# Row statistics by two ScalarE passes, turns from 128 rows, and a new order of instructions, in a gated linear attention with an MLP

## The chip, the cores and the metric

The kernel runs on one core of one Trainium2 chip. The time is that of the device, in microseconds, and the median of 3 runs of the kernel before is 220.5 us (219.09 to 223.66). Engines are named as in the profile: PE is TensorE, DVE VectorE, ACT ScalarE, POOL GpSimd, SP SyncE. A profile comes from one further execution, whose own time is given with it.

## The reference

Batch 4, 8 heads, 768 steps, 48 columns a head; x has 4 x 768 rows of 384 columns.

```python
def _attn_ref(q, k, v, a_re, a_im):
    mag = np.sqrt(a_re * a_re + a_im * a_im)
    scale = np.minimum(mag, 0.999) / (mag + 1e-06)
    a_re_n, a_im_n = (a_re * scale, a_im * scale)
    for t in range(S):
        new_re = ar * S_re - ai * S_im
        new_im = ar * S_im + ai * S_re
        S_re, S_im = (new_re + outer(k[t], v[t]), new_im)
        y[:, :, t] = np.einsum('bhd,bhde->bhe', q[:, :, t], S_re)

def _moe_ref(x, g_ln, w_ch1, w_ch2):
    mu = np.mean(x, axis=-1, keepdims=True)
    var = np.mean((x - mu) ** 2, axis=-1, keepdims=True)
    xn = (x - mu) / np.sqrt(var + 1e-06) * g_ln
    return x + np.maximum(xn @ w_ch1, 0.0) @ w_ch2
```

## The kernel before

The 4 x 768 rows are cut into 24 chunks of 128 rows (six a batch). Chunks are worked in 9 groups: chunk 0, chunks 1 and 2, and then seven groups of three. Per group, the gates come first. Under one ACT table (natural log and exp), `gate_exp` takes the log of a_re, the ratio r = a_im / a_re, and from both the log of the magnitude (lm), which is capped; a matmul with a triangular matrix sums it down the rows (`l_ps`), and two exp passes give the factors `epn`. Under the other table (trig), `gate_trig` takes the arctangent of r; matmuls sum the angles in turns (`th_ps`), and ACT takes sine and cosine. The whole group's q and k are multiplied by the factors (`qke`, L581) and by sine and cosine (`stk`, L587). The two tables alternate, 12 loads of them in all (L369). The first phase (a pair of loads) holds the first two groups, the second to fourth one group each, and the last two two groups each.

Per chunk, `attention` turns q and k (on PE for chunks 0 to 11, by DMA from SP for 12 to 23), takes the scores (`a_ps`), masks them (`at`), gets `y_ps` from them, v and the carried state s, and copies it to `x` in bf16 (L669). `feed` takes mean and variance of each row of x (L723, L724), turns x (`x_ps`, `xt`), multiplies by the first weights (`h_ps`), applies relu (`ht`, L767 on ACT and L769 on DVE), multiplies by the second weights (`o_ps`), scales by the reciprocal root of the variance (`rs`, three chunks at once, on POOL, L728 and L729), adds x (L786) and stores. The mean is taken out in the weights themselves: at the start `centre` is built from g_ln, and `fold` multiplies it into the first weights.

Nothing is scheduled by the program at run time: every operation is an entry of a plan, and two tables fix what happens. `HOW` names the engine of each of the operations that have a choice (V is DVE, A is ACT, P is POOL; a string has one letter for each group, chunk, or half of a chunk), and its `'order'` (L51) lists the numbers of all 806 operations in the order in which they are emitted. Each engine, and each queue of DMAs on SP and POOL, works off its own part of that list strictly in order. `'fill'` (L89) says before which results PE runs idle matmuls with the identity (`filled`, L173). The microseconds in `op`, `opt` and `act` are the planner's costs; they do nothing when `'order'` is given.

The lines that the change touches:

- L723 and L724: `bn_stats` and `bn_aggr` on DVE, whose second column of `mv` is the variance; L728 adds 1e-6 to it, L729 raises it to -0.5.
- L669: the copy of `y_ps` to `x`, on ACT for 10 chunks and on DVE for 14.
- L529: the whole turns. A matmul of a one-row tile `ones` with a one-row tile `rows` (192 turns, or 768 for chunks 3 to 5 of the first batch) starts each sum of angles, and L531 and L533 add to it with 128-row matrices. L262 and L263 fill `rows`.
- L738: the copy of `x_ps` to `xt`, on DVE.

Of the kernel before, what the change touches and what calls it, by code (L numbers as in the profile page):

```python
# [10 lines left out]
FP32 = mybir.dt.float32  # L11
# [37 lines left out]
 'xt': 'PPPPPPPPPPPPDDDDDDDDDDDD',  # L49
 'qkt': 'PPPPPPPPPPPPDDDDDDDDDDDD',  # L50
 'order': [12, 27, 41, 221, 13, 10, 23, 11, 25, 4, 1, 7, 35, 15, 5, 37, 59, 57, 53, 202, 222, 223, 51, 234, 209, 235,  # L51
# [37 lines left out]
 'fill': {209: 6.42, 229: 1.25, 242: 0.23, 249: 2.72, 494: 0.37, 496: 1.33, 779: 0.34}}  # L89
# [35 lines left out]
def kernel(  # L125
# [38 lines left out]
    def filled(ps):  # L164
# [5 lines left out]
        else:  # L170
            n = min(ps.shape[1], 512) // C
            for _ in range(int(us / (0.003 + n * 0.0534))):
# [13 lines left out]
             (2, ("dec",)), (4, ("edge",)), (6, ("carry",))] + [(2, ("in_" + n,)) for n in ("ar", "ai", "q", "k", "v")]  # L186
# [38 lines left out]
    def load(eng, g0, g1, names, after=()):  # L225
        b, c0, c1 = g0 // NCH, g0 % NCH, g0 % NCH + g1 - g0
        us = 0.6 if eng is Y else 0.66 + 0.26 * (c1 - c0)
# [50 lines left out]
    def constants():  # L278
# [5 lines left out]
        for name, us, fn, a in (("ones", 0.17, plain, (1.0,)),  # L284
                                ("all_turn", 0.17, plain, (INV2PI,)), ("all_back", 0.17, plain, (-INV2PI,)),
                                ("near", 0.86, shifts, (0, 192.0)), ("far", 0.86, shifts, (32, 768.0))):
            op(V, us, [], [("c_" + name,)], fn, name, *a)
        op(V, 0.23, [("c_u_turn",), ("c_all_turn",)], [("c_back",)], back)
        op(V, 0.3, [], [("c_small",)], small)
# [93 lines left out]
    def gate_exp(G):  # L383
# [67 lines left out]
        fp = lambda p: dict(V=0.48, A=0.52, P=p)  # L451
# [6 lines left out]
        if ratio:  # L458
# [3 lines left out]
            each("r", dict(V=0.48, P=0.95), ["ai"], [("rec", g)], "r", e_r, [in_("ai")])  # L462
            opt("r2", g, dict(V=0.06 + 0.215 * n, A=sb, P=0.06 + 0.69 * n), [("r", g)], [("r2", g)], e_r2, port=True)
            act(sb, [("r2", g), ("c_small",)], [("m2", g)], e_l1p, uses=[("rec", g)])
            op(V, 0.06 + 0.42 * n, [("ln", g), ("m2", g)], [("lm", g)], e_both, uses=[rw], port=True)
        else:
            each("ar2", fp(0.82), ["ar"], [], "ar2", e_ar2, [in_("ar")])
            each("ai2", fp(0.82), ["ai"], [], "m2", e_ai2, [in_("ai")])
            each("m2", dict(V=0.48, P=0.95), [], [("ar2", g), ("m2", g)], "sum", e_m2, [in_("ar")])
            act(sb, [("ar2", g)], [("ln", g), rw], e_ln, uses=[in_("ar")])  # L470
            act(sb, [("ln", g)], [("rw", rw[1], "rec")], e_rec, uses=[rw])
            each("r", dict(V=0.48, P=0.95), ["ai"], [("rw", rw[1], "rec")], "r", e_r, [in_("ai"), rw])
# [13 lines left out]
    def gate_trig(G):  # L486
# [20 lines left out]
        for j in (js[::-1] if G["back"] else js):  # L507
# [4 lines left out]
            elif (j != js[0] if G["back"] else j != js[-1]) or (G["b"] == 0 and G["c0"] + j < NCH - 1):  # L512
                key = ("carry", next(sums))
                opt("carry", c, dict(V=0.36, P=0.36), [last[1], ("th", g)], [key], e_add, last[0], j, key, port=True, **kw)
                last = ((lambda key=key: cell[key]), key)
# [340 lines left out]
```

## Time and profile before

| what | us |
|---|---|
| median of 3 runs | 220.5 |
| time of the profiled execution | 218.88 |
| its span | 217.1 |
| POOL busy (93 instructions) | 100.9 |
| 12 ACT table loads, each | 1.283 |
| granted PE clock, mean | 0.976 |
| masking of scores, L641, 24 of DVE | 29.1 |

The span runs from the first to the last instruction. Busy time of an engine is the time in which one of its instructions was running. A row of a group gives the count, the busy time, the mean duration of one in ns, and the idle time of the engine just before them with what ended it. The chain is found by going back from the last instruction, at each step to whatever released it, so that its pieces add up to the span.

### The profile page before, as it was taken

What the parts mean: (1) busy time and instruction counts of PE and PEld (TensorE: products, weight loads), DVE (VectorE), ACT (ScalarE), POOL (GpSimd) and SP (SyncE); (2) the same over time, 40 slices, a digit from 0 to 9 for tenths busy, and PEclk for the clock granted to TensorE, in tenths of its full rate; (3) what the DMA queues carried; (4) which work ended last, traced back from release to release, by engine and by line L of the source; (5) the groups of instructions that cost most, each with busy time, mean ns of one, the idle gap of its engine ahead of it and who ended that gap; (6) DMA issues with size and microseconds to landing.
All of it is one profiled execution on the core that took longest, in us unless ns stands there. A gap on an engine that the chain in (4) does not pass through costs nothing.

```text
span 217.1 us, 5425 instructions
## 1 busy us (share of the span) xinstructions
PE 187.7 (86%) x2292; PEld 134.6 (62%) x2295; DVE 177.9 (82%) x297; ACT 128.9 (59%) x161; POOL 100.9 (46%) x93
## 2 busy tenths in 40 slices
PE   3997695879789989997988889787999999899992
PEld 1333342658666976757866646567876677787871
DVE  4372779799999898999999967997968998888671
ACT  2259674929778797939988867528698511110100
POOL 4089997494966976346992800760060100020200
PEclk9999979999999999999999957999999999999999
DMA  6999999999799999999999929798349499792202
GB/s 109 180 165 109 189 150 157 145 198 156 65 143 139 215 180 202 189 143 248 162 78 201 198 27 211 135 146 136 92 101 138 92 219 177 182 156 57 92 3 109
DMA packets 136885, 31.45 MB, mean 145 GB/s; under 512 B 129948, under 2 KB 135772, under 8 KB 136860
## 3 DMA queue, kind: packets, MB, share of 16 engines
q0 software_dynamic: 78192, 14.16, 84.8%
q1 hardware_dynamic: 58668, 16.93, 39.2%
q8 instruction: 18, 0.29, 0.6%
q14 instruction: 7, 0.06, 0.1%
HBM read 28.31 MB, written 4.72 MB: 152 GB/s over the span
## 4 chain that ended last, share of the span: by engine, by line
PE 34%; DVE 27%; ACT 12%; DMA 11%; POOL 5%; issue 5%; SPq 3%; DVEq 0%; ACTq 0%; POOLq 0%
PE o_ps L782 13%; PE h_ps L761 11%; DMA qkt<-stk 5%; DVE at L641 5%; DVE lm L424 3%; SPq L214 3%; DVE w L546 3%; DMA ai<-in_a_im_dram 2%; DVE stk L587 2%; ACT epn L442 2%; ACT r L492 2%; DMA out_dram<-o 2%; DVE ht L769 2%; DMA xt<-x 2%; DVE r L390 2%
## 5 line engine op out<-in xcount | busy, mean ns | idle before, releaser
L761 PE MATMUL h_ps<-xt,w1c 128*128 128x128 bf16 x864 | 55.4, 220 | 2.8 <-DMA xt<-x 1.3
L761 PEld LDWEIGHTS <-w1c 128*128 128x128 bf16 x864 | 50.6, 98 | 4.6 <-issue 2.4
L782 PE MATMUL o_ps<-w2b,ht 128*128 128x384 bf16 x288 | 51.5, 331 | 0.0
L782 PEld LDWEIGHTS <-ht 128*128 128x128 bf16 x288 | 27.6, 99 | 17.3 <-issue 1.2
L767 ACT ACTIVATE ht<-h_ps 128x1024 bf16<-128x1024 f32 (+1 forms) x30 | 24.1, 820 | 23.4 <-PE h_ps L761 14.4
L641 DVE TENSOR_TENSOR at<-a_ps,mask 128x1024 bf16<-128x1024 f32 x24 | 29.1, 1216 | 2.8 <-PE a_ps L637 2.6
L728 POOL TENSOR_SCALAR rs<-mv 128x3 f32<-128x3 f32 x8 | 3.7, 464 | 56.0 <-DVE mv L724 37.2
L390 POOL TENSOR_TENSOR r<-ai,m 128x384 bf16<-128x384 f32 x13 | 13.5, 1058 | 21.8 <-ACT m L411 12.7
L442 ACT ACTIVATE epn<-l_ps 128x384 bf16<-128x384 f32 (+1 forms) x32 | 18.6, 658 | 6.2 <-PE l_ps L437 6.2
L786 DVE SCALAR_TENSOR_TENSOR o<-o_ps,rs,x 128x384 f32<-128x384 f32 x24 | 14.6, 613 | 8.9 <-PE o_ps L782 4.8
L769 DVE TENSOR_SCALAR ht<-h_ps 128x512 bf16<-128x512 f32 (+1 forms) x18 | 16.5, 921 | 1.8 <-PE h_ps L761 1.7
L581 POOL TENSOR_TENSOR epn<-qk,epn 128x1152 bf16<-128x1152 bf16 (+2 forms) x7 | 14.4, 2064 | 7.5 <-ACT epn L442 7.0
L637 PE MATMUL a_ps<-qkt 128*128 128x128 bf16 x192 | 14.8, 220 | 3.4 <-DMA qkt<-stk 2.0
L612 PE MATMUL qk_ps<-ident,stk 128*128 128x128 bf16 x192 | 13.4, 219 | 4.8 <-DVE stk L587 4.5
L369 ACT ACT_TABLE_LOAD x12 | 15.4, 1283 | 0.9 <-PEq L840 0.7
L612 PEld LDWEIGHTS <-stk 128*128 128x128 bf16 x192 | 11.4, 98 | 6.7 <-DVE stk L587 5.4
L546 DVE TENSOR_SCALAR w<-th_ps 128x384 f32<-128x384 f32 (+1 forms) x16 | 11.7, 749 | 4.2 <-ACT sin L543 4.1
L637 PEld LDWEIGHTS <-qkt 128*128 128x128 bf16 x192 | 11.6, 98 | 5.6 <-DMA qkt<-stk 2.2
L663 PE MATMUL y_ps<-v,at 128*128 128x48 bf16 x192 | 12.4, 183 | 1.8 <-DVE at L641 1.8
L173 PEld LDWEIGHTS <-ident 128*128 128x128 bf16 x55 | 6.2, 117 | 12.4 <-issue 5.3
L408 ACT ACTIVATE rec<-ar 128x1152 f32<-128x1152 f32 (+2 forms) x9 | 9.4, 1054 | 7.4 <-DMA ar<-in_a_re_dram 7.4
L543 ACT ACTIVATE sin<-th_ps 128x384 bf16<-128x384 int16 (+1 forms) x14 | 8.8, 645 | 8.0 <-PE th_ps L533 6.2
(102 smaller groups left out, 374.2 us busy)
## 6 DMA issues: line engine op xcount, KB each, us to landing
out_dram<-o SPq DMA_DIRECT2D x24, 192.0 KB, 7.0
ai<-in_a_im_dram SPq DMA_DIRECT2D x12, 192.0 KB, 5.0
ar<-in_a_re_dram SPq DMA_DIRECT2D x12, 192.0 KB, 7.0
ar<-in_a_re_dram POOLq DMA_DIRECT2D x2, 1152.0 KB, 13.4
ai<-in_a_im_dram POOLq DMA_DIRECT2D x2, 1152.0 KB, 12.1
qk<-in_k_dram POOLq DMA_DIRECT2D x3, 576.0 KB, 10.6
qk<-in_q_dram POOLq DMA_DIRECT2D x3, 576.0 KB, 10.8
v<-in_v_dram POOLq DMA_DIRECT2D x3, 576.0 KB, 8.6
```

The costliest lines, as they stand in the source:

```text
L369: op(A, 1.28, old, [key], lambda: A.preload_act_table_set(TABLES[which]))
L390: times = lambda eng, out, x, y: eng.tensor_tensor(out=out, in0=x, in1=y, op=ALU.mult)
L442: A.activation(out=o, in_=banks(G["l_ps", j], m), func=AF.Exp, scale=(1.0, -1.0)[s])
L546: V.tensor_scalar(out=cols(f32(G, "w"), j, m), in0=banks(G["th_ps", j], m), scalar1=0.25, scalar2=None, op0=ALU.add)
L612: T.transpose(ps[:, h], G["stk"][:, int(which == "ks"), j, ts(h, C)], K["ident"])
L637: T.matmul(ch["a"][:, h], lhsT=ch["kt"][:, h], rhs=ch["qt"][:, h], start=True, stop=True)
L641: V.tensor_tensor(out=ch["at"], in0=ch["a"], in1=K["mask"].unsqueeze(1).to_broadcast([C, H, C]), op=ALU.mult)
L761: T.matmul(ps[:, jj], lhsT=w1c[:, i, ts(j0 + jj, C)], rhs=ch["xt"][:, i], start=(i == 0), stop=(i == ND - 1))
L767: A.activation(out=o, in_=i, func=AF.Relu)
L769: V.tensor_scalar(out=o, in0=i, scalar1=0.0, scalar2=None, op0=ALU.max)
L782: T.matmul(ps, lhsT=ch["ht"][:, i], rhs=w2b[:, i], start=(i == 0), stop=(i == NJ - 1))
L786: V.scalar_tensor_tensor(out=ch["o"], in0=ch["o_ps"], scalar=stats[u, "rs"][:, ds(j, 1)], in1=ch["x"], op0=ALU.mult, op1=ALU.add)
```

## The change

The row statistics leave DVE. The copy of `y_ps` to `x` is now always made by ACT and gives the sum of the row as a side result; a second ACT pass squares (sum - 384 x) and sums that, the bias being the sum of the first pass. The sum of squares is 384 cubed times the variance, which the first instruction of `rs` divides out. The copy to `xt` may be on ACT (it is for chunks 0, 1 and 4). The turns come from one column of a 128-row tile `base` (1.5 in each row, so that 128 of them make 192, or 6.0 for 768), repeated over 384 columns, times the 128-row `ones`. The rings of q and k, which share a tile, are one in the plan. Planner costs are changed, engines are chosen anew, and order and fillers are new. The loads and their queues are the same; their order in the queues is not.

On SP the first loads (a_re as ar, a_im as ai, each with its chunk) were ai1, ar0, ar1, ar2, ai0, ai2, ar5, ai4, ai3, ar3, then the first two `edge` DMAs, then ar4 and ai5; now they are ai1, ar1, ar0, ai0, ar2, ai2, ar4, ar3, the two `edge` DMAs, and then ai5, ai3, ar5 and ai4. On POOL u_half was built right behind the first r, ahead of all q and k loads; now u_turn, one weight load and three q loads come between.

```diff
- 'r2': 'VVVVVAPPAVVVVVVVVVVVVVVV',
- 'r': 'PVVVVVVPVPPPPPPVVVPPPPVP',
- 'carry': 'VVPVPVVPVVPVVPVVVVVVVVVV',
- 'fold': 'AAAAAAAAV',
+ 'r2': 'VVVVVAVAAVVVVVVVVVVVVVVV',
+ 'r': 'PVVVVVVVVPPPPPPVPVPVVVVP',
+ 'carry': 'VPVVPVVPVVPVVVVVPVVPVVVV',
+ 'fold': 'VAVVAVAAA',
...
- 'x': 'VVAVVAAVVAAVVVAAVAAVVVAV',
- 'qt': 'AVVVAVVVAVVVAAAAAAAAAAAA',
- 'kt': 'VVVVAVVVAVVAVVVVVVVVVVVV',
- 'relu': 'AVAAAVAVAAAAAAAAAAVAAVVAAAAVAVAVAAVAAVVAVVVAVAVV',
- 'qk': 'PVPVPPPPVVVVVPVVVVVVVVVVVVVVVVVVVVVVVVVVVVVVVVVV',
+ 'qt': 'VAVVAVVAVVVVAAAAAAAAAAAA',
+ 'kt': 'AAVVAVVVAVVAVVVVVVVVVVVV',
+ 'relu': 'AAVAAVAVVAAVVVAAAAAAVVAAAAAVVAVVAAAVVAAAAAVAAAVA',
+ 'qk': 'VPVVPVPPVPVVVVPPVVVVVVVVVVVVVVVVVVVVVVVVVVVVVVVV',
+ 'stk': 'VVVVVVVVVVVVVVVVVVVVVVVVVVVVVVVVVVVVVVVVVVVVVVVV',
...
+ 'xc': 'AAVVAVVVVVVVVVVVVVVVVVVV',
...
- 'fill': {209: 6.42, 229: 1.25, 242: 0.23, 249: 2.72, 494: 0.37, 496: 1.33, 779: 0.34}}
+ 'fill': {212: 0.53, 228: 7.0, 248: 2.41, 491: 0.34}}
...
-    rows = consts.tile([34, DM], BF16, name="rows")
-
-    def shifts(name, at, turns):
-        K[name] = rows[at:at + 2]
-        V.memset(K[name], 0.25)
-        V.memset(rows[at:at + 1], turns)
+    def turn_base():
+
+        K["base"] = consts.tile([C, 4], BF16, name="base")
+        for at, each_, first in ((0, 1.5, 1.5), (1, 1.5, 1.75), (2, 6.0, 6.0), (3, 6.0, 6.25)):
+            V.memset(K["base"][:, at:at + 1], each_)
+            if first != each_:
+                V.memset(K["base"][0:1, at:at + 1], first)
...
-                at = 32 if G["far"] else 0
-                T.matmul(o, lhsT=K["ones"][at:at + 1 + more], rhs=rows[at:at + 1 + more].rearrange(
-                    "p (h d) -> p h d", h=H), start=True, stop=False)
+                at = 2 * G["far"] + more
+                T.matmul(o, lhsT=K["ones"], rhs=K["base"][:, at:at + 1].unsqueeze(2).to_broadcast([C, H, D]),
+                         start=True, stop=False)
...
-        def x_out(eng):
+        def x_out():
+
             ch["x"] = moe.tile([C, DM], BF16, tag="x", name="x", bufs=5)
-            (A.copy if eng is A else V.tensor_copy)(out=ch["x"], in_=ch["y"])
+            if u not in stats:
+                stats[u] = att.tile([C, GMAX, 2], FP32, tag="mv", name="mv")
+            A.activation(out=ch["x"], in_=ch["y"], func=AF.Copy, accum_out=stats[u][:, g % GMAX, 0:1])
...
-        opt("x", g, dict(A=0.49, V=0.5), [("y_ps", g)], [("x", g)], x_out)
+        op(A, 0.65, [("y_ps", g)], [("x", g), ("mv", u)], x_out)
...
-        def bn():
-            if u not in stats:
-                stats[u] = att.tile([C, GMAX, 2], FP32, tag="mv", name="mv")
-            s6 = att.tile([C, 6], FP32, tag="s6", name="s6")
-            V.bn_stats(out=s6, in_=ch["x"])
-            V.bn_aggr(out=stats[u][:, j], in_=s6)
+        def spread():
+
+            A.activation(out=junk, in_=ch["x"], func=AF.Square, scale=-float(DM), bias=stats[u][:, j, 0:1],
+                         accum_out=stats[u][:, j, 1:2])
...
-            P.tensor_scalar(out=t, in0=stats[u][:, :, 1], scalar1=1e-6, scalar2=None, op0=ALU.add)
+            P.tensor_scalar(out=t, in0=stats[u][:, :, 1], scalar1=1.0 / DM ** 3, scalar2=1e-6, op0=ALU.mult, op1=ALU.add)
...
-        def xt_out():
+        def xt_out(eng):
             ch["xt"] = moe.tile([C, ND, C], BF16, tag="xt", name="xt")
-            V.tensor_copy(out=ch["xt"], in_=ch["x_ps"])
+            (A.copy if eng is A else V.tensor_copy)(out=ch["xt"], in_=ch["x_ps"])
...
-        op(V, 0.75, [("x", g)], [("mv", u)], bn)
+        op(A, 0.68, [("x", g)], [("sq", g), ("mv", u)], spread)
```

The two lists under `'order'`, some 800 numbers each, are left out; what of them matters is said above and where it is used.

More of the change, by code (lines that the diff above doesn't have):

```diff
@@ L185 @@
              (2, ("sin",)), (2, ("cos",)), (2, ("stk",)), (2, ("mv",)), (2, ("rs",)),
-             (2, ("dec",)), (4, ("edge",)), (6, ("carry",))] + [(2, ("in_" + n,)) for n in ("ar", "ai", "q", "k", "v")]
+             (2, ("dec",)), (4, ("edge",)), (6, ("carry",))] + [(2, ("in_" + n,)) for n in ("ar", "ai", "v")] + [
+        (2, ("in_q", "in_k"))]
     plan = Plan(RINGS, SLOTS)
@@ L226, in load @@
         b, c0, c1 = g0 // NCH, g0 % NCH, g0 % NCH + g1 - g0
-        us = 0.6 if eng is Y else 0.66 + 0.26 * (c1 - c0)
+        us = 0.5 if eng is Y else 0.66 + 0.26 * (c1 - c0)
         for n in names:
@@ L284, in constants @@
         for name, us, fn, a in (("ones", 0.17, plain, (1.0,)),
-                                ("all_turn", 0.17, plain, (INV2PI,)), ("all_back", 0.17, plain, (-INV2PI,)),
-                                ("near", 0.86, shifts, (0, 192.0)), ("far", 0.86, shifts, (32, 768.0))):
+                                ("all_turn", 0.17, plain, (INV2PI,)), ("all_back", 0.17, plain, (-INV2PI,))):
             op(V, us, [], [("c_" + name,)], fn, name, *a)
         op(V, 0.23, [("c_u_turn",), ("c_all_turn",)], [("c_back",)], back)
+        op(V, 0.42, [], [("c_base",)], turn_base)
         op(V, 0.3, [], [("c_small",)], small)
@@ L450, in gate_exp @@
         in_ = lambda x: ("in_" + x, G["b"])
-        fp = lambda p: dict(V=0.48, A=0.52, P=p)
+        fp = lambda p: dict(V=0.55, A=0.52, P=p)
         def each(name, costs, x, needs, make, fn, uses):
@@ L461, in gate_exp @@
             act(sb, [("ln", g)], [("rec", g)], e_rec, uses=[rw])
[L462 to L465, printed above, removed]
+            each("r", dict(V=0.56, P=1.02), ["ai"], [("rec", g)], "r", e_r, [in_("ai")])
+            opt("r2", g, dict(V=0.11 + 0.215 * n, A=sb, P=0.06 + 0.69 * n), [("r", g)], [("r2", g)], e_r2, port=True)
+            act(sb + 0.1, [("r2", g), ("c_small",)], [("m2", g)], e_l1p, uses=[("rec", g)])
+            op(V, 0.12 + 0.415 * n, [("ln", g), ("m2", g)], [("lm", g)], e_both, uses=[rw], port=True)
         else:
@@ L468, in gate_exp @@
             each("ai2", fp(0.82), ["ai"], [], "m2", e_ai2, [in_("ai")])
-            each("m2", dict(V=0.48, P=0.95), [], [("ar2", g), ("m2", g)], "sum", e_m2, [in_("ar")])
+            each("m2", dict(V=0.56, P=1.02), [], [("ar2", g), ("m2", g)], "sum", e_m2, [in_("ar")])
             act(sb, [("ar2", g)], [("ln", g), rw], e_ln, uses=[in_("ar")])
             act(sb, [("ln", g)], [("rw", rw[1], "rec")], e_rec, uses=[rw])
-            each("r", dict(V=0.48, P=0.95), ["ai"], [("rw", rw[1], "rec")], "r", e_r, [in_("ai"), rw])
+            each("r", dict(V=0.56, P=1.02), ["ai"], [("rw", rw[1], "rec")], "r", e_r, [in_("ai"), rw])
             act(sb, [("sum", g)], [("lm", g)], e_lm, uses=[("m2", g)])
-        op(V, 0.06 + 0.13 * n, [("lm", g)], [("cap", g)], e_cap, port=True)
+        op(V, 0.15 + 0.14 * n, [("lm", g)], [("cap", g)], e_cap, port=True)
         for j, m in pairs(G):
@@ L513, in gate_trig @@
                 key = ("carry", next(sums))
-                opt("carry", c, dict(V=0.36, P=0.36), [last[1], ("th", g)], [key], e_add, last[0], j, key, port=True, **kw)
+                opt("carry", c, dict(V=0.36, P=0.92), [last[1], ("th", g)], [key], e_add, last[0], j, key, port=True, **kw)
                 last = ((lambda key=key: cell[key]), key)
@@ L552, in gate_trig @@
             turn = 0.05 + 0.17 * (2 * m + len(bs)) + 0.3 * (m - 1)
-            op(T, turn, [("th", g), ("c_back",), ("c_all_back",), ("c_ones",), ("c_far" if G["far"] else "c_near",)] + bs, [("th_ps", g, j)], e_phase, j, m, 0, takes="wide", **kw)
+            op(T, turn, [("th", g), ("c_back",), ("c_all_back",), ("c_ones",), ("c_base",)] + bs, [("th_ps", g, j)], e_phase, j, m, 0, takes="wide", **kw)
             ps, half, got_sin = ("th_ps", g, j), 0.13 + 0.42 * m, ("sin", g, j)
@@ L586, in e_stack @@
             G["stk1"] = o.rearrange("p (c m) d -> p c (m d)", c=n)
-            V.tensor_tensor(out=o.rearrange("p (c s h a) d -> p c s h a d", s=2, h=H, a=2)[:, :, :, :, i, 0:D],
+            eng.tensor_tensor(out=o.rearrange("p (c s h a) d -> p c s h a d", s=2, h=H, a=2)[:, :, :, :, i, 0:D],
                             in0=both(G, "epn")[:, 0:2].rearrange("p s (c h d) -> p c s h d", h=H, d=D),
@@ L593, in gate_trig @@
         for s in range(2):
-            opt("qk", 2 * g + s, dict(V=0.1 + 0.215 * n, P=0.1 + 0.75 * n), got("qk"[s]) + [(("ep", "en")[s], g)],
+            opt("qk", 2 * g + s, dict(V=0.14 + 0.215 * n, P=0.13 + 0.75 * n), got("qk"[s]) + [(("ep", "en")[s], g)],
                 [("qke", g)], e_qk, s, uses=[("in_" + "qk"[s], G["b"]), ("epn", g)], port=True)
         for i in range(2):
-            op(V, 0.1 + 0.405 * n, [("qke", g), (("sin", "cos")[i], g), ("c_stk", g % 2)], [("stk", g)], e_stack, i,
-               uses=[("epn", g)], port=True)
+            opt("stk", 2 * g + i, dict(V=0.14 + 0.405 * n, P=0.13 + 1.5 * n), [("qke", g), (("sin", "cos")[i], g), ("c_stk", g % 2)],
+                [("stk", g)], e_stack, i, uses=[("epn", g)], port=True)
     chunks = {g: {} for g in range(NG)}
+    stats = {}
     state = [None]
@@ L607, in attention @@
         b, c = divmod(g, NCH)
+        u = g // GMAX
         def heads(which):
@@ L627, in attention @@
         if HOW["qkt"][g] == "D":
[L628 removed]
+            over_sp(1.95, 2.5, 1.4, [("stk", G["i"])], [("qt", g), ("kt", g)], heads_dma)
         else:
@@ L742, in xt_dma @@
             Y.dma_start_transpose(out=ch["xt"], in_=ch["x"])
-        op(V, 0.75, [("x", g)], [("mv", u)], bn)
+        op(A, 0.68, [("x", g)], [("sq", g), ("mv", u)], spread)
         if j == GMAX - 1:
-            op(P, 1.2, [("mv", u), ("c_small",)], [("rs", u)], rs)
+            op(P, 1.3, [("mv", u), ("c_small",)], [("rs", u)], rs)
         if HOW["xt"][g] == "P":
             op(T, 0.2, [("x", g)], [("x_ps", g)], x_turn, takes="nar")
-            op(V, 0.36, [("x_ps", g)], [("xt", g)], xt_out)
+            opt("xc", g, dict(A=0.49, V=0.36), [("x_ps", g)], [("xt", g)], xt_out)
         else:
@@ L775, in feed @@
             m = j1 - j0
-            opt("relu", 2 * g + (j0 > 0), dict(A=0.17 + 0.107 * m, V=0.08 + 0.137 * m), [("h_ps", g, j0)], [("ht", g)],
+            opt("relu", 2 * g + (j0 > 0), dict(A=0.17 + 0.107 * m, V=0.16 + 0.132 * m), [("h_ps", g, j0)], [("ht", g)],
                 relu, j0, j1)
@@ L808 @@
             load({"Y": Y, "P": P}[eng], g0, g1, LOADS[what])
-    op(V, 2.2, [("gln",), ("c_ident",), ("c_ones",)], [("centre",)], centring, port=True)
+    op(V, 2.3, [("gln",), ("c_ident",), ("c_ones",)], [("centre",)], centring, port=True)
     for n in range(DF // 512):
```

7 lines of the change are left out of this document (3 added, 4 removed), and 74 rows, old and new, of the table HOW.

## The prediction

> **What bounds the kernel now.** I read the page's busy times first, then the busy time by stretch, then the chain that ended last, then the groups by shape, then single rows of TensorE.
>
> ```profile
> PE 187.7 (86%) x2292; PEld 134.6 (62%) x2295; DVE 177.9 (82%) x297; ACT 128.9 (59%) x161; POOL 100.9 (46%) x93
> ```
>
> No engine is full over the span, so the average decides nothing. The stretches are cut where the second table pair begins (25.76 us), at the last table load (160.60) and at the last matmul (213.20):
>
> ```profile
> 0.00:25.76 25.76, 18.34 (x72) 7.53 (x73) 12.38 (x35) 13.71 (x20) 16.03 (x25) 1.00 1.24 148
> 25.76:160.60 134.84, 118.78 (x1568) 88.91 (x1571) 121.14 (x194) 100.02 (x122) 80.62 (x63) 0.96 1.47 154
> 160.60:213.20 52.60, 50.60 (x656) 38.13 (x652) 43.74 (x70) 15.12 (x20) 4.23 (x7) 1.00 0.76 123
> ```
>
> Columns: PE, PEld, DVE, ACT, POOL. In the middle DVE is the fullest (121.1 of 134.8, 90%), PE next (118.8); in the tail PE is packed (50.6 of 52.6) and ACT nearly idle. The chain agrees that DVE and PE share the end:
>
> ```profile
> PE 34%; DVE 27%; ACT 12%; DMA 11%; POOL 5%; issue 5%; SPq 3%; DVEq 0%; ACTq 0%; POOLq 0%
> ```
>
> The prices come from the groups by shape:
>
> ```profile
> L723 DVE BATCH_NORM_STATS2 s<-x 128x6 f32<-128x384 bf16 x24 | 13.2, 548 | 0.0
> L724 DVE BATCH_NORM_AGGREGATE mv<-s 128x2 f32<-128x6 f32 x24 | 4.4, 182 | 0.8
> L669 DVE CAST x<-y_ps 128x384 bf16<-128x384 f32 x14 | 7.6, 549 | 0.3 <-PE y_ps L665 0.2
> L669 ACT CAST x<-y_ps 128x384 bf16<-128x384 f32 x10 | 4.8, 478 | 12.0 <-PE y_ps L665 7.5 <-PE y_ps L663 4.5
> L408 ACT ACTIVATE rec<-ar 128x384 f32<-128x384 f32 x1 | 0.5, 522 | 4.9 <-DMA ar<-in_a_re_dram 4.9
> L421 ACT ACTIVATE m<-lm,one 128x384 f32<-128x384 bf16 x1 | 0.6, 615 | 1.8 <-DVE lm L390 1.8
> ```
>
> **Part 1, statistics and x.** DVE loses 24 bn_stats (13.2 us), 24 bn_aggr (4.4) and 14 copies of x (7.6): 25.2 us. ACT gains 14 copies and 24 squares. An ACT pass over 384 columns is 0.478 us from PSUM, 0.522 from SBUF; a per-partition bias adds 0.093 (615 against 522). The trace has no ACT sum: its price lies between 0 and the 0.182 of a bn_aggr, also a tiny write; I take 0.093, the nearest ACT row with one more small operand. So x costs 0.571 and a square 0.708: 24 x 0.571 - 4.8 + 24 x 0.708 = +25.9 us (21.4 to 30.2).
>
> **Part 2, engines swapped.** On ACT: two kt copies (+2.0, at 1.005), three xt copies (+1.4), one r2 (+1.2), three net fold copies fewer (-1.8, at 0.59), relu level: +3 us. On DVE these, with r (+1.8), r2 (+0.8), fold (+2.0) and memsets (-1.2), cancel to about 0. POOL loses some 6 us. Totals: DVE 153, ACT 158.
>
> **Part 3, turns from 128 rows.** Each of 24 chunks adds its turns by a one-row matmul (L529):
>
> ```profile
> 70.23 0.32 PE L533 MATMUL th_ps<-carry,all_back 128*128 128x384 bf16 x1
> 70.49 0.33 PE L529 MATMUL th_ps<-rows,ones 1*128 1x384 bf16 x1
> 70.75 0.34 PE L531 MATMUL th_ps<-r,u_back 128*128 128x384 bf16 x1
> 70.92 0.33 PE L533 MATMUL th_ps<-r,all_back 128*128 128x384 bf16 x1
> ```
>
> Starts are 0.26 apart into and out of the one-row matmul and 0.17 between two of 128 rows. The weight loads beside them show why: the one after a one-row load idles 0.17 on "issue" and starts with its matmul instead of ahead of it. With 128 rows everywhere I price both at 0.17: 0.2 us less PE a chunk, 4.7 in all. That the new moving operand repeats one column of SBUF has no row; from 0 to the 4.7 us given back. The Trainium skill (TensorE: Matmul & The Clock Gate, "LDWEIGHTS (loading the stationary operand)") says a load's time goes by its columns and not by the contraction rows. The loads' own durations agree (91 ns with one row, 97 with 128); if that were all, this part would be worth nothing.
>
> **Part 4, the order.** Front: the two fold copies that stood in the chain between epn of the first two groups (0.97 us at 16.70) leave ACT there, but the second group's l_ps matmuls are ready only at 17.00 to 17.3, so about 0.35 is won. Against it, POOL now issues one weight load and three q loads (0.79 + 3 x 0.9) and writes u_turn (0.57) before u_half, which the first l_ps needs; after r at 11.60 that is 17.2 instead of 13.2. But ai of chunk 0 moves from fifth to fourth on SP's queue, about 1.3 us earlier at 192 KB and 145 GB/s, which leaves l_ps at some 16, against 15.47, still ahead of the second group. Bounds -1.0 to +1.5. DVE's centre (2.3 us) moves behind cap, into its idle time up to 21.7; without that cover it costs 2.3. The PE fillers go from 12.7 to 10.3 us, all where PE waits for the gates: nothing. Of the large loads one k load (2.25 us of POOL) goes behind r of the fifth group; r at 79.0 was released by a DMA, so I count nothing (0 to -2.3). SP's four last small a loads now stand behind the edge DMAs at 16.7; they are needed at 28.4 and landed in 5 to 7: nothing, up to +2 if late.
>
> The new wait is that of rs on POOL, for ACT's third square of a unit instead of DVE's bn_aggr; behind rs on POOL stand v loads and r of the next group, which the chain passes from 52.67 to 60.0. The square stands ahead of the next table load on ACT, so I take the same time; 1.3 more if it came behind that load.
>
> **The sum.** Front -0.35. Middle: the chain in order of time holds five bn_stats pieces (0.46 to 0.48) and three bn_aggr (0.18), 2.9 us; the last pair, ahead of rs at 52.67, only turns into a square on ACT, so 2.25 goes. It holds 17 th pieces of L529 and L531 at 0.27 or more, 0.105 less each: 1.8. Two x pieces stay, dearer by 0.1 each. Together -3.9: 130.9. Loads allow that: ACT rises to 100.0 + 16 squares (11.3) + 17 x for 7 (6.4) + swaps (4) less overlap of neighbours (0.09 each, two 499 ns epn passes take 0.87) = 119.4, or 91% of 130.9; over 100 to 120 us ACT has held 18.8 of 20. Tail: 8 th pieces give 0.84, and DVE, 9 to 12 us lighter, should let PE win half of its 2.0 idle: -1.8. Last residual and store unchanged. 218.9 - 6.1 = 212.8 in terms of the profiled execution, whose own time (218.88) is 1.6 below the median of the runs; that gives 214 for the median.
>
> **Rivals.**
> - **ACT takes DVE's place, nothing is won** (0.22). For: 119 us in 134.8 is where DVE stood (121), and ACT works in order. Packed at 88%, the middle is 135.7; with the front and 1.3 of the tail 218.1, or 219.7 by the median. Against: DVE and PE both become lighter. The Trainium skill (ScalarE: Activation LUTs, "Rules for kernel authors") points this way: simple elementwise work belongs on VectorE, up to about three times faster in bf16. For x this trace says otherwise (478 against 549 ns); for a square from SBUF it agrees (DVE takes 346 for 384 bf16, ACT 522).
> - **The one-row gap stays** (0.05): the column read again and again is as slow. Then 2.6 us of the sum go: 217. This is also what the skill's rule on load time would give.
> - **ACT's queue holds x back** (0.16), slower. Place: the stages of chunks 3 to 17, where x of 10 chunks came from DVE and now stands behind table loads (1.28), ln and exp passes (1.16) and squares on ACT; x_ps, xt and h_ps then wait, and PE behind them in order. ACT was already idle for 35 us of the middle, behind others. It decides below a packing of 84% (119 / 141.6 = +6.8, above +2% in all); at 82% the middle is 145 and the median 228.
> - **Squares reload tables** (0.02), slower. The trace shows Square (L394) under the exp table only. 17 of 24 squares stand under the trig table; for the 9 of them in the middle two loads of 1.283 each add 23 us to ACT's 119; at 91% packing the middle is 156 and the whole some 240. The Trainium skill (ScalarE: Activation LUTs, "Table sets: the hidden batching unit") names relu, copy, identity and abs as in every set, and says a load is put before an activation that needs one.
>
> **How the numbers follow.** The forecast gets 0.55, by itself 208 to 216. A run of this kernel can be told from no change at about 2% (the three runs spread over 2%): below 216.1 is faster, above 224.9 slower. Faster 0.55; within 2%, the two middle rivals, 0.22 + 0.05 = 0.27; slower 0.16 + 0.02 = 0.18. The range takes in the two middle rivals and the open prices (ACT sum ±4, front, k load): 207.5 to 223.
>
> **What would show it.** Right: DVE near 153 and ACT near 158 busy, squares near 0.71, x near 0.57, th matmuls 0.17 apart, the middle near 131, no more than 12 table loads, the chain with more ACT and no bn. Wrong: PE idle ahead of x_ps, xt or h_ps released by ACT x; ACT over 92% full without a shorter middle; th starts still 0.26 apart; l_ps of the first groups after 18.

## The result, and the profile after

The changed kernel takes 213.16 us (median of 4 runs, 211.1 to 214.93), the kernel before 220.44 beside it (219.09 to 223.66). The ratio is 0.9625, 95% interval 0.9552 to 0.9699. Ratios, here and below, leave out the slow executions (those more than 1.5% above the fastest of their kernel, one of 358.51 us of `order_only` among them), so they are not the quotients of the medians. The profiled execution, 214.6 us with a span of 212.7 (before: 218.88 and 217.1), is one of the longer ones. What is read from it by stretch holds for this execution. A second set of runs gave 0.9576 (0.9524 to 0.9627).

The page's busy times of the changed kernel, to be held against the first line shown in the prediction:

```profile
PE 182.5 (86%) x2285; PEld 135.0 (63%) x2285; DVE 155.0 (73%) x237; ACT 153.2 (72%) x251; POOL 96.5 (45%) x89
```

DVE gave up 22.9 us, ACT took 24.3, PE gave up 5.2. The busy time by stretch of the changed kernel, cut at the same events as before (second table pair, last table load, last matmul); the columns are PE, PEld, DVE, ACT, POOL, PE clock, DMA share and GB/s:

```profile
0.00:26.35 26.35, 17.36 (x63) 6.94 (x63) 11.56 (x39) 12.99 (x19) 16.86 (x27) 0.94 1.22 155
26.35:157.85 131.50, 115.34 (x1557) 89.32 (x1558) 111.60 (x158) 114.17 (x181) 71.10 (x55) 0.95 1.45 156
157.85:208.90 51.05, 49.82 (x667) 38.72 (x664) 31.19 (x41) 26.05 (x52) 8.60 (x9) 1.00 0.80 131
```

The front is 0.6 longer by this cut (the table load itself starts at 26.27, 0.5 later than before), the middle 3.3 shorter, the tail 1.55 shorter. In the middle ACT, DVE and PE now stand at 87, 85 and 88%: none is full. The chain that ended last, by engine and by line:

```profile
PE 35%; ACT 22%; DMA 18%; DVE 17%; issue 3%; SPq 2%; POOL 1%; ACTq 0%; DVEq 0%
PE o_ps L788 18%; PE h_ps L767 9%; DMA w2b<-in_moe_w_ch_dram 8%; DMA ar<-in_a_re_dram 6%; DMA xt<-x 4%; ACT m L424 4%; ACT epn L445 4%; DVE stk L590 4%; DVE w L549 3%; ACT L372 2%; PE a_ps L642 2%; ACT r L495 2%; ACT sin L546 2%; SPq L216 2%; PE qk_ps L617 2%
```

ACT has taken DVE's place on the chain (12 to 22%), as the forecast had it. Not forecast is the growth of DMA from 11 to 18%, with one piece of the second weights, w2b, alone at 8%. The chain in order of time shows that piece:

```profile
42.93 16.16 DMA w2b<-in_moe_w_ch_dram
59.13 2.72 PE o_ps L788 x8
```

POOL issues the third part of the second weights at 42.93, and it lands 16.16 us later. In the kernel before, no such part took over 10.1 us, and PE never waited for one. What PE does around it, in stretches of 1 us (same columns):

```profile
54.00:55.00 1.00, 0.00 (x0) 0.00 (x0) 1.00 (x3) 1.00 (x2) 1.00 (x2) 1.00 1.27 192
55.00:56.00 1.00, 0.00 (x0) 0.00 (x0) 0.89 (x2) 1.00 (x2) 1.00 (x2) 0.84 1.27 181
56.00:57.00 1.00, 0.50 (x2) 0.28 (x3) 0.00 (x0) 0.49 (x1) 1.00 (x1) 0.50 1.26 183
...
59.00:60.00 1.00, 0.87 (x3) 0.41 (x3) 0.68 (x2) 0.00 (x0) 0.00 (x0) 0.50 2.52 142
...
62.00:63.00 1.00, 1.00 (x16) 1.00 (x15) 0.29 (x1) 0.00 (x0) 0.00 (x0) 0.75 2.70 143
63.00:64.00 1.00, 1.00 (x10) 0.61 (x7) 1.00 (x2) 0.84 (x1) 0.00 (x0) 1.00 2.70 142
```

PE is empty from 53.6 to 56.5, works off four matmuls, and is empty again until 59.13 (4.0 us of waits for w2b). The granted clock falls to 0.50 at about 55.7, that is 2.1 us into the first hole, and comes back only about 62.5. So in this execution the late load costs PE its 4.0 us and then half the speed of some 3.4 us of packed work. The Trainium skill (TensorE: Matmul & The Clock Gate, "What's actually happening") says that an idle window of about 3.4 us halves TensorE's clock until a busy one has passed. The trace agrees on the size, 0.50, and on the return, 3.4 us from 59.13 to 62.5; it differs on the idle time, since a hole of 2.9 us was enough.

In the front the trace shows the same on a smaller scale. The first two rows are of the changed kernel, the third of the kernel before (PE's timeline; fillers are matmuls with the identity):

```profile
16.07 0.73 PE L440 MATMUL l_ps<-lm,u_half 128*128 128x384 bf16 x3 [3.27 <-POOL u_half masks.py:66]
17.37 4.14 PE L174 MATMUL th_ps<-ident 128*128 128x512 bf16 x11 [0.57 <-ACT epn L445]
17.33 2.75 PE L173 MATMUL th_ps<-ident 128*128 128x512 bf16 x12
```

PE waits 3.27 us for u_half, the clock stands at 0.50 from about 18 to 21.5, and eleven fillers take longer than twelve did before. They hold back the first matmul that adds r to the angles: it starts at 21.59, while r was ready at about 20.6 (an estimate: r's pass starts at 20.02, and before that matmul started 0.57 after such a start, at 20.97).

The prices of the two new passes, from the groups by shape (count, busy time, mean ns):

```profile
L729 ACT ACTIVATE junk<-x,mv 128x384 bf16<-128x384 bf16 x24 | 14.7, 614 | 0.2
L677 ACT ACTIVATE x<-y_ps 128x384 bf16<-128x384 f32 x24 | 11.7, 490 | 10.9 <-PE y_ps L670 5.4 <-issue 4.0 <-PE y_ps L668 1.5
L677 ACT ACTIVATION_READ_ACCUMULATOR x<-y_ps 128x1 f32 x24 | 4.9, 203 | 0.0
L729 ACT ACTIVATION_READ_ACCUMULATOR junk<-x,mv 128x1 f32 x24 | 4.7, 196 | 0.0
```

The sum is an instruction of its own, some 0.2 us long. In ACT's timeline (start, length, both in us) the reads and their neighbours overlap:

```profile
71.88 0.47 ACT L677 ACTIVATE x<-y_ps 128x384 bf16<-128x384 f32 x1
72.25 0.19 ACT L677 ACTIVATION_READ_ACCUMULATOR x<-y_ps 128x1 f32 x1
72.47 0.61 ACT L729 ACTIVATE junk<-x,mv 128x384 bf16<-128x384 bf16 x1
73.00 0.19 ACT L729 ACTIVATION_READ_ACCUMULATOR junk<-x,mv 128x1 f32 x1
73.09 0.47 ACT L677 ACTIVATE x<-y_ps 128x384 bf16<-128x384 f32 x1
```

From start to start x takes 0.59 and a square 0.62. The turns, from PE's timeline of the changed kernel:

```profile
164.92 0.32 PE L532 MATMUL th_ps<-base,ones 128*128 128x384 bf16 x1
165.08 0.32 PE L534 MATMUL th_ps<-r,u_turn 128*128 128x384 bf16 x1
165.24 0.32 PE L532 MATMUL th_ps<-base,ones 128*128 128x384 bf16 x1
165.41 0.33 PE L534 MATMUL th_ps<-r,u_turn 128*128 128x384 bf16 x1
```

All starts are 0.16 to 0.17 apart, where those beside a one-row matmul were 0.26. There are still 12 table loads.

### The profile page after: what moved, and what is told of

Same layout as the page of the kernel before. It is cut to its first block, busy times and chain, and to the rows that moved or that the text cites. A ratio compares the mean times of both kernels' runs of the same rounds, so it can differ in the third digit from the quotient of the medians.

```text
span 212.7 us, 5443 instructions
## 1 busy us (share of the span) xinstructions
PE 182.5 (86%) x2285; PEld 135.0 (63%) x2285; DVE 155.0 (73%) x237; ACT 153.2 (72%) x251; POOL 96.5 (45%) x89
## 4 chain that ended last, share of the span: by engine, by line
PE 35%; ACT 22%; DMA 18%; DVE 17%; issue 3%; SPq 2%; POOL 1%; ACTq 0%; DVEq 0%
PE o_ps L788 18%; PE h_ps L767 9%; DMA w2b<-in_moe_w_ch_dram 8%; DMA ar<-in_a_re_dram 6%; DMA xt<-x 4%; ACT m L424 4%; ACT epn L445 4%; DVE stk L590 4%; DVE w L549 3%; ACT L372 2%; PE a_ps L642 2%; ACT r L495 2%; ACT sin L546 2%; SPq L216 2%; PE qk_ps L617 2%
## 5 line engine op out<-in xcount | busy, mean ns | idle before, releaser
L788 PE MATMUL o_ps<-w2b,ht 128*128 128x384 bf16 x288 | 53.6, 340 | 4.4 <-DMA w2b<-in_moe_w_ch_dram 4.0
L767 PE MATMUL h_ps<-xt,w1c 128*128 128x128 bf16 x864 | 53.8, 219 | 1.3 <-DMA xt<-x 1.1
L773 ACT ACTIVATE ht<-h_ps 128x512 bf16<-128x512 f32 (+1 forms) x31 | 24.4, 800 | 7.6 <-PE h_ps L767 7.2
L775 DVE TENSOR_SCALAR ht<-h_ps 128x1024 bf16<-128x1024 f32 (+1 forms) x17 | 16.5, 969 | 8.3 <-PE h_ps L767 8.2
L584 POOL TENSOR_TENSOR epn<-qk,epn 128x1152 bf16<-128x1152 bf16 (+1 forms) x7 | 15.1, 2158 | 15.5 <-ACT epn L445 15.5
L677 ACT ACTIVATE x<-y_ps 128x384 bf16<-128x384 f32 x24 | 11.7, 490 | 10.9 <-PE y_ps L670 5.4
L393 POOL TENSOR_TENSOR r<-ai,m 128x384 bf16<-128x384 f32 x10 | 10.4, 1060 | 12.6 <-ACT m L414 12.6
L424 ACT ACTIVATE m<-lm,one 128x1152 f32<-128x1152 bf16 (+2 forms) x9 | 10.2, 1148 | 6.8 <-DVE lm L393 5.3
L729 ACT ACTIVATE junk<-x,mv 128x384 bf16<-128x384 bf16 x24 | 14.7, 614 | 0.2
L174 PEld LDWEIGHTS <-ident 128*128 128x128 bf16 x45 | 5.2, 117 | 13.2 <-issue 6.8
```

The lines of the kernel that those rows point to most:

```text
L424: A.activation(out=f32(G, "m2"), in_=flat(G, "lm"), func=AF.Ln, bias=K["one"])
L584: eng.tensor_tensor(out=o, in0=part(G, "qk"[s]).rearrange("p h c d -> p c h d"), in1=i, op=ALU.mult)
L767: T.matmul(ps[:, jj], lhsT=w1c[:, i, ts(j0 + jj, C)], rhs=ch["xt"][:, i], start=(i == 0), stop=(i == ND - 1))
L773: A.activation(out=o, in_=i, func=AF.Relu)
L775: V.tensor_scalar(out=o, in0=i, scalar1=0.0, scalar2=None, op0=ALU.max)
L788: T.matmul(ps, lhsT=ch["ht"][:, i], rhs=w2b[:, i], start=(i == 0), stop=(i == NJ - 1))
```

## The experiments

Ratios are to the kernel before, run beside each kernel on the same chip; its medians there were 221.33, 221.55 and 222.45 us. Intervals are of 95%.

### The three parts, one by one

The change has three parts that can be put in or left out on their own: the statistics (and x) on ACT, the turns from 128 rows, and the new order with its engines. Eight kernels hold all combinations; six of them are experiments.

`one_row` is the changed kernel with the turns from one row:

```diff
-        for at, each_, first in ((0, 1.5, 1.5), (1, 1.5, 1.75), (2, 6.0, 6.0), (3, 6.0, 6.25)):
+        for at, each_, first in ((0, 192.0, 192.0), (1, 192.0, 192.25), (2, 768.0, 768.0), (3, 768.0, 768.25)):
...
-                T.matmul(o, lhsT=K["ones"], rhs=K["base"][:, at:at + 1].unsqueeze(2).to_broadcast([C, H, D]),
+                T.matmul(o, lhsT=K["ones"][0:1], rhs=K["base"][0:1, at:at + 1].unsqueeze(2).to_broadcast([1, H, D]),
```

> The changed kernel with the whole turns from one row again (192 or 768 in one row, one column repeated), everything else as changed. Theory (the one-row weight load costs 0.2 us of PE per chunk, 4.7 in all, and about half of it lies on the path): th starts go back from 0.16 to about 0.26 apart, and the time rises by 2 to 3 us, ratio to the kernel before 0.972 to 0.978. Rival (PE has 30 us of idle time and swallows it): th starts 0.26 apart, but the ratio stays at 0.96 to 0.966.

`bn_back` is the changed kernel with the statistics on DVE, at the places where the squares stood; x stays on ACT, without its sum:

```diff
-            A.activation(out=ch["x"], in_=ch["y"], func=AF.Copy, accum_out=stats[u][:, g % GMAX, 0:1])
+            A.copy(out=ch["x"], in_=ch["y"])
...
-            A.activation(out=junk, in_=ch["x"], func=AF.Square, scale=-float(DM), bias=stats[u][:, j, 0:1],
-                         accum_out=stats[u][:, j, 1:2])
+            V.bn_stats(out=s6, in_=ch["x"])
+            V.bn_aggr(out=stats[u][:, j], in_=s6)
...
```

The lines left out give `rs` the variance as in the kernel before, and the plan the new engine.

> The changed kernel with mean and variance by bn_stats and bn_aggr on DVE again, at the places of the squares in the new order; x is still copied by ACT, without its sum. Theory (what was won is the relief of DVE): DVE back to some 173 us busy, ACT down to some 134, and the time rises by 3 to 5 us, ratio 0.976 to 0.985. Rival (the new order wins the time, whoever does the statistics): ratio 0.96 to 0.967.

`order_only` has both of these edits, so that only order and engines are new (all copies of x on ACT among them):

> The changed kernel with both other parts undone: bn_stats and bn_aggr on DVE, turns from one row; what is left is the new order and choice of engines (all copies of x on ACT). Theory (the parts add up: order and engines about 0.5% by themselves, the turns 0.9, the squares on ACT 2.2): ratio 0.99 to 1.0. Rival (the turns only help where DVE is relieved): 0.98 to 0.987, the same as with bn_stats and 128-row turns.

`b_turns` is the kernel before with the turns from 128 rows (a column of 1.5 or 6.0, repeated, as in the change), `b_stats` the kernel before with x, its sum and the squares on ACT, the turns from one row of a repeated column, and `b_both` has the two together:

```diff
-  'x': 'VVAVVAAVVAAVVVAAVAAVVVAV',
+  'x': 'AAAAAAAAAAAAAAAAAAAAAAAA',
...
-            (A.copy if eng is A else V.tensor_copy)(out=ch["x"], in_=ch["y"])
+            A.activation(out=ch["x"], in_=ch["y"], func=AF.Copy, accum_out=stats[u][:, g % GMAX, 0:1])
...
-            V.bn_stats(out=s6, in_=ch["x"])
-            V.bn_aggr(out=stats[u][:, j], in_=s6)
+            A.activation(out=junk, in_=ch["x"], func=AF.Square, scale=-float(DM), bias=stats[u][:, j, 0:1],
+                         accum_out=stats[u][:, j, 1:2])
...
```

> The kernel before, in its own order, with the whole turns from 128 rows (1.5 or 6.0 in one column of each row, repeated). Theory: PE 4.7 us lighter, of which 2.6 were on the chain: ratio 0.985 to 0.99. Rival (DVE sets the pace, PE's gain becomes idle time): 0.997 to 1.0.

> The kernel before, in its own order, with the statistics of the change: all copies of x on ACT with their sums, and the squares on ACT at the places of bn_stats; turns from one row of one repeated column. Theory (DVE relief is worth something even in an order that was not made for it): DVE 153, ACT 155, ratio 0.98 to 1.0. Rival (without a new order ACT holds x back behind its passes): above 1.005.

> The order and the engines of the kernel before, with x, its sum and the squares on ACT and with the turns of 128 rows; it completes the ladder of eight kernels (statistics old or new, turns old or new, order old or new). Theory, the parts of the change add: statistics 1.033 and turns 0.991 give 1.033 x 0.991 = 1.024. Rival: turns from 128 rows are worth more where ACT holds PE up, or nothing there because PE has slack: 1.033 if nothing, below 1.018 if more. In either case it stays above 1, so that moving the statistics costs time unless order and engines are made for it.

| statistics | turns | order before | new order |
|---|---|---|---|
| DVE | one row | 1 | 0.983 (0.976 to 0.990), `order_only` |
| DVE | 128 rows | 0.991 (0.987 to 0.995), `b_turns` | 0.985 (0.977 to 0.992), `bn_back` |
| ACT | one row | 1.033 (1.026 to 1.041), `b_stats` | 0.971 (0.962 to 0.980), `one_row` |
| ACT | 128 rows | 1.017 (1.011 to 1.023), `b_both` | 0.9625 (0.955 to 0.970), the change |

Three things follow. First, moving the statistics to ACT costs time in the old order (0.991 to 1.017 with 128-row turns, intervals far apart) and saves it in the new one (0.985 to 0.9625, apart as well). The two steps are not quite the same edit: in the old order it also takes 14 copies of x from DVE to ACT, which in the new order are on ACT on both sides. No run moves these copies alone, so how much of the loss is theirs stays open. Second, the turns are worth 0.9% alone, shown, and 1.6% where the statistics are on ACT in the old order (1.033 to 1.017); in the new order the step they make is smaller than the intervals. Third, the parts don't add: 1.017 (both in the old order) x 0.983 (the order alone) is 1.000, where the whole change gives 0.9625. (1.033 x 0.991 is 1.024, just above the interval of `b_both`; with the noise of both factors this one shows nothing.)

Held against what was expected: `b_turns` came out just above its theory's range, `b_stats` and `order_only` as their rivals had it, `bn_back` at the upper end of its theory, `b_both` as the half of its rival in which the turns are worth more there. The interval of `one_row` takes in theory and rival.

Where the time goes in the old order is in the busy time by stretch of `b_stats`, middle and tail (same columns):

```profile
24.85:166.24 141.39, 121.48 (x1566) 89.84 (x1567) 107.83 (x153) 113.34 (x179) 78.61 (x63) 0.94 1.42 147
166.24:221.43 55.19, 53.85 (x660) 39.59 (x657) 36.55 (x48) 23.18 (x49) 5.18 (x7) 0.94 0.74 116
```

and in two of its largest waits (total, times, longest):

```profile
ACT x L669 <- PE y_ps L662: 15.0, 5, 6.3
...
DVE o L783 <- POOL rs L726: 8.4, 4, 4.2
```

ACT holds the same load as in the changed kernel (113.3 against 114.2 us in the middle), but in 141.4 us: it is packed at 80%, not at 87%. Ahead of its copies of x ACT waits 21.8 us in all for y_ps, against 12.0 in the kernel before, which has 10 of them there, and 6.9 in the changed kernel; DVE's residual waits 8.4 us for `rs`, which comes behind the squares (1.3 us in the kernel before). PE gains nothing from a DVE that is 21 us lighter: its busy time rises by 5.2 us, at a lower granted clock (0.70 from 176 to 186 us, where the tail before stood at 1.00). That these waits of ACT and DVE are what slows PE is likely, not shown: of PE's own waits in `b_stats` none is for ACT's x, and 0.2 us is for the residual behind `rs`.

### Is ACT the bound now?

`no_square` is the changed kernel without the squares; `rs` is then 1, so it leaves out the scaling by the variance:

```diff
-            A.activation(out=junk, in_=ch["x"], func=AF.Square, scale=-float(DM), bias=stats[u][:, j, 0:1],
-                         accum_out=stats[u][:, j, 1:2])
+            pass
...
-            P.tensor_scalar(out=t, in0=stats[u][:, :, 1], scalar1=1.0 / DM ** 3, scalar2=1e-6, op0=ALU.mult, op1=ALU.add)
+            P.tensor_scalar(out=t, in0=stats[u][:, :, 0], scalar1=0.0, scalar2=1.0, op0=ALU.mult, op1=ALU.add)
```

> The changed kernel without the squares: rs is 1 for every row, the rest as changed (the rows are not scaled by their variance). ACT is about 17 us lighter. Theory (ACT has become the fullest engine of the middle, 114 of 131.5 us, and shares the end with PE): 2 to 4 us faster than the change, ratio 0.945 to 0.955. Rival (the squares lie beside PE's work and cost nothing): 0.96 to 0.965.

It gave 212.44 us, 0.9551 (0.9483 to 0.9619). ACT's busy time fell by 13.4 us, from 153.2 to 139.8, and the time by less than the intervals can tell from the change (0.9625 and 0.9576). The result lies between theory and rival and decides between them only so far: 13.4 us less of ACT bring between nothing and some 3 us (an estimate, from 0.9625 to the low end, 0.9483), so ACT's load as a whole is not what bounds the changed kernel. The run prices the pieces too: 13.4 / 24 is 0.56 us of ACT for a square, and 139.8 against the 137.7 of `bn_back`, which has neither squares nor sums, is 0.09 us for a sum beside x.

### The load that came late

In the changed kernel POOL issues two loads of q and k of the second batch (576 KB each) ahead of the second and third part of w2b. `kq_late` moves both behind the third group's multiplication of q and k; `kq_late_uhalf` also writes u_half directly behind the first r, ahead of what stands on POOL between:

```diff
- 267, 110, 493,  ...  278, 117, 501,  ...  299, 292,
+ 267, 493,  ...  278, 501,  ...  299, 110, 117, 292,
```

> The changed kernel with one more change of order: the q and k loads of the second batch (576 KB each) are issued by POOL behind the loads of the second weights, not ahead. Theory (the second weights took 16 us to land behind those two in POOL's DMA queue, 16 us of the chain, and PE waited 4.0 us for them): they land in 7 to 10, o_ps of chunk 0 starts near 53 instead of 56.5, and the time falls by 1 to 3 us, ratio 0.949 to 0.958. Rival (the next wait, ACT's or DVE's in the same stretch, takes its place): 0.960 to 0.965.

> As the last, and u_half written by POOL right behind the first r, ahead of u_turn and four DMA issues. Theory (PE waited 3.3 us for u_half, and ACT's first epn starts with it at 16.45): the first epn starts near 15.3, the four run without a gap until some 18.1 instead of 18.73, and 0.5 us is won on top, if the a loads behind the edge DMAs come earlier with it: 0.947 to 0.956. Rival (the a loads of chunks 3 to 5 behind the edge DMAs set the second phase): no difference to the last.

Neither was faster than the change: 0.978 (0.972 to 0.984), slower, and 0.969 (0.963 to 0.975), which overlaps the change's first interval. The busy time by stretch of `kq_late` shows the hole at another place:

```profile
50.00:60.00 10.00, 9.37 (x123) 7.65 (x121) 9.42 (x13) 8.85 (x11) 5.58 (x4) 1.00 2.85 145
60.00:70.00 10.00, 7.17 (x105) 5.12 (x104) 9.32 (x12) 6.86 (x12) 7.54 (x7) 1.00 2.36 125
70.00:80.00 10.00, 5.71 (x62) 5.22 (x61) 5.41 (x7) 5.38 (x12) 4.49 (x2) 0.71 1.27 209
```

w2b lands in 5.3 to 6.6 us and PE is busy for 9.37 of 10 us where it was busy for 5.62; but now PE waits 4.3 us for a v load and POOL 9.1 for a_im, PE's hole lies at 70 to 80, and the clock falls there. The packets of POOL's queue take 84 to 85% of the span of 16 engines, before and after the change; in this execution, putting these loads back moved the wait instead of removing it.

`w2_early` moves one load by little: the k load (117) goes right behind the last part of w2b (70). `uhalf` moves only u_half, and `after_again`, the changed kernel as it is, stands beside them:

```diff
- 278, 117, 501,  ...  215, 70, 300,
+ 278, 501,  ...  215, 70, 117, 300,
```

> The changed kernel with one load moved: the 576 KB k load of the second batch that was issued ahead of the last load of the second weights is issued right behind it; nothing else is changed. Theory: the landing of the second weights (16.2 us after issue, PE waits 4.0 us for it at 56.50 and 59.13) is a matter of what stands in POOL's software queue before it, so they land some 3 us earlier, and the middle is shorter by 1 to 3 us: ratio 0.950 to 0.958. Rival: the queue is full throughout (83 to 84 percent of the span of 16 engines), so that the load that is put back is late where it is needed, as with the two loads put back before (0.978): 0.962 to 0.978, with PE idle later instead, between 70 and 80 us.

> The changed kernel with one operation moved: u_half, the half triangle that the first l_ps matmuls need, is written by POOL directly behind the first r, ahead of u_turn and of the weight load and three q loads that stood before it; nothing else is changed. Theory: POOL's queue holds the first l_ps back (u_half was written at 16.02 us; without the five entries it would be at about 13.5), so PE's 3.3 us wait for it becomes shorter, epn of the first group starts 1 to 2 us earlier, and the first two stretches end earlier; beside the kernel with the late q and k loads the same move took the ratio from 0.978 to 0.969. That gives 0.955 to 0.960 here. Rival: the chain at 26.3 us ends in a tie with the landing of a_re of the second phase (26.33, behind the edge DMAs on SP), so the front keeps its length and POOL's q loads only land later: 0.961 to 0.966, as the change itself.

> The changed kernel itself, as the neighbour of the two runs that move one operation each, so that all three stand on one chip. Expected 0.955 to 0.970 of the kernel before, whose interval was 0.955 to 0.970; a chip-to-chip difference above 0.005 would say that ratios from different calls can't be compared to less than that.

Landings and waits are those of the one profiled execution of each:

| kernel | median of 6 runs | ratio | landing of the three parts of w2b, least / median / most | PE waits for it |
|---|---|---|---|---|
| `after_again` | 212.47 | 0.9576 (0.9524 to 0.9627) | 5.7 / 15.9 / 16.6 | 4.5 |
| `uhalf` | 214.0 | 0.9553 (0.9476 to 0.9629) | 5.9 / 16.3 / 16.6 | 4.8 |
| `w2_early` | 210.94 | 0.9503 (0.9440 to 0.9565) | 5.3 / 5.3 / 5.9 | 0 |

In the profiled execution of `w2_early` the wait is gone, and the hole does not come back elsewhere to the same size:

```profile
50.00:60.00 10.00, 9.29 (x100) 6.85 (x98) 8.88 (x12) 8.39 (x10) 5.55 (x5) 1.00 2.00 139
60.00:70.00 10.00, 6.71 (x115) 4.93 (x114) 9.03 (x14) 7.50 (x14) 7.74 (x6) 1.00 2.15 144
70.00:80.00 10.00, 9.72 (x180) 9.36 (x177) 9.41 (x14) 9.55 (x14) 6.05 (x5) 1.00 0.91 233
```

What is left is 3.3 us of idle time of PE at 60 to 70, in four pieces without a fall of the clock; 1.0 us of it is for a v load that lands 8.35 us after its issue at 61.20. The middle of this execution is 126.9 us, against 131.6 in the changed kernel. It has the lowest ratio of the study, and is faster than the kernel before beyond doubt; that it beats the changed kernel is likely, not shown, since the intervals of 0.9503 and 0.9576 overlap by 0.004.

The wait isn't there in every kernel with the same order of loads. w2b landed in at most 12.2 us in the profile of `one_row` and 8.7 in that of `no_square`, and PE waited for it in neither; in that of `bn_back` it took 16.3 and PE waited 4.3 us. This looks like a race in a full queue, which one execution can lose and another win, but no kernel has a profile of each kind, and these kernels differ in other edits. So that the moved load is what freed w2b in `w2_early` is likely, not shown. Both profiled executions of the changed kernel lie above its medians and have the wait; whether its shorter runs (211.1) are those without it has no profile to show.

`uhalf` did not do what it was for. The first group's `epn` began at 15.90 instead of 16.45, but PE's wait for u_half turned into waits for lm from DVE, the second group's `epn` moved from behind the first to 17.75, and the second table pair began at 27.11 instead of 26.27 (r itself came 0.5 later in this execution). The clock fell to 0.50 here too, from about 15 to 21.8, and the eleven fillers took 4.66 us. u_half wasn't alone in holding the front.

## Why the prediction was right, and where it was wrong

The likeliest case came true, with 214.0 forecast and 213.16 measured, by faster passes than priced, a wait that wasn't seen, and an order that was worth more than was counted. That the number is so near is in part luck: two misses of the sum run against each other. In terms of the profiled execution, in which the sum was made, 212.8 was forecast and 214.6 came.

- **What bounded the kernel** (DVE and PE together in the middle, PE in the tail): right, with a limit. Taking DVE's load away is worth nothing by itself (`b_stats`), so the 90% of DVE was not a bound that a lighter DVE lifts by itself; the order had to go with it.
- **Part 1, prices.** The sum was taken at 0.093, and is 0.09 net. The square was priced at 0.708 and occupies 0.62 from start to start, 0.56 by `no_square`: as if only one of its two small operands were paid for; the overlap seen in the timeline would do that, but no run separates them. ACT came to 153.2 where 158 was forecast, DVE to 155.0 where 153 was.
- **Part 3, turns.** Starts 0.16 to 0.17 apart, and PE's busy time is 5.0 us less than in `one_row` (182.5 against 187.5), and 4.8 less in `b_turns` than before (182.9 against 187.7); 4.7 was forecast. Alone it gives 0.9%, 1.9 us by `b_turns`, where the sum had 1.8 + 0.84. The rival that the gap stays is out, and with it the reading by which load time alone would make this part worth nothing: the loads' durations are alike, but neither the one-row load nor the one behind it starts ahead of its own matmul (70.48 and 70.75 in the kernel before, with matmuls at 70.49 and 70.75).
- **Part 4, the front**, forecast at -0.35: wrong in sign in the profiled execution, +0.5. l_ps began at 16.07, as priced ("at some 16"), and the first load of the trig table at 18.73 instead of 19.10, so the 0.35 was won there. It was lost again behind that load. The step that failed is the one on the fillers, "all where PE waits for the gates: nothing". At half the clock, behind PE's wait for u_half, they held the first matmul with r until 21.59; in `w2_early`, where they ended sooner, that matmul started at 21.14, and the second pair began at 25.82 instead of 26.27. In the second profile of the changed kernel it was 21.03 and 25.71, even with the kernel before (25.76). Part of the loss has another cause: ACT now takes the first chunk's sine behind its cosine, ahead of the next sine. SP's small a loads behind the edge DMAs, which were given "nothing, up to +2 if late", cost nothing here: the last a_re landed at 26.33, and ACT was loading its table from 26.27 to 27.55.
- **Part 4, the large loads**, "I count nothing (0 to -2.3)": this step left out what the profiles then showed. It asked what the moved k load does to r at 79, and not which other loads the new order of the queue makes late. That was w2b, in both profiled executions of the changed kernel, with 4.0 us of PE waits and a half clock behind them in the first.
- **Part 4, the order as such** was given 0.35 in the front and nothing elsewhere; the 1 us of the tail beyond the turns was put down to a lighter DVE. `order_only` puts order and choice of engines together at 1.7% (1.0 to 2.4%), 3.7 us. This term was mis-sized. In the new order the statistics then bring 0.983 to 0.971, some 2.6 us, where the sum had 2.05 and that 1 in the tail, and the turns 0.971 to 0.9625, 1.9 us. These last two steps are smaller than the intervals.
- **The middle**, 130.9 forecast, 131.5 measured with the late load in it, 126.9 in an execution of `w2_early` without it. As far as these two executions show, counting pieces of the chain gave the right size because two errors cancel, the late load that wasn't seen and the order that was worth more. That is luck.
- **The tail**, -1.8 forecast, -1.55 measured; the cause given for half of it doesn't hold. `bn_back`, with 36.2 us of DVE in its tail instead of 31.2, has a tail of 50.7, as the change has (51.05). So it was not the lighter DVE that packed PE; the order and the turns remain (`one_row`: 51.7), each by a single execution.
- **ACT takes DVE's place**: seen in the chain (22%) and at 87% of the middle, but `no_square` leaves it between nothing and some 3 us.
- **ACT's queue holds x back**: the time of `b_stats` is like this rival's. The point named was a packing of 84%; `b_stats` stands at 80% and is 3.3% slower, where 82% was said to give 228 us; it took 228.34. But its sign, PE idle ahead of x_ps, xt or h_ps released by ACT's x, isn't in the waits of `b_stats`, and its middle is 141.4 us where the rival had 145, so the agreement of 228 is luck in part, and the mechanism isn't shown. With the new order the time did not come to this.
- **Squares reload tables**: out, 12 loads in all.

## What to carry to other kernels

Whether moving work from a fuller engine to an emptier one pays can hang on the order of instructions: moving the statistics, with 14 copies of x, cost 2.6% in the old order, and moving the statistics saved 2.3% in the new one. When an order changes, list for each full DMA queue not only what a moved load needs, but which loads now stand behind it and when each is first read. A wait of PE of about 3 us (2.9 and 3.3 here) should be priced with the half clock behind it, and fillers behind such a wait are not free.

## What was not expected of the hardware

- ACT's sum of a row is a separate instruction of 0.196 to 0.203 us that starts about 0.1 before the pass ends; a pass with it delays the next by 0.09 us.
- A 384 KB load through POOL's queue took 5.1 to 16.4 us to land in one execution, and in kernels with the same order of loads its longest landing was 8.7, 12.2 or 16.4.
- A PE hole of 2.9 us was enough to bring the granted clock to 0.50, 2.1 us after it began; with a second hole of 1.2 us inside the stretch at 0.50, the half clock lasted some 6.8 us, from about 55.7 (0.84 as the mean of that microsecond) to 62.5 (0.75).
